# Attention's token sums tied three a step behind the evacuation, and one weight split five steps later

## The chip, the core and the metric

The kernel runs on one core of a Trainium2 chip. The metric is the device time of one execution in microseconds (us). The core has TensorE (matrix products, PE in the rows), VectorE (DVE), ScalarE (ACT), GpSimd (POOL) and SyncE (SP), which issues most DMA transfers. Each engine works through its own list of instructions in order; an instruction waits for those on other engines that it depends on, and all behind it on its engine wait with it.

## What is computed

Causal attention with a decay, then a layer of four weighted two-layer networks, then a gated two-layer network, all in float32:

```python
B, H, S, D = 2, 8, 576, 64
scores = q @ k.T / sqrt(D) + (cum[:, None] - cum[None, :])   # cum = cumsum(log(clip(f, 1e-4, 1))), causal mask
x = softmax(scores) @ v                                     # to tokens: (1152, 512)
p = domain_probs / domain_probs.sum(-1)
x = sum(p[:, e] * (relu(x @ w1[e]) @ w2[e]) for e in range(4))   # w1: 512 x 1024, w2: 1024 x 512
h = x @ w_in                                                # 512 x 2048
out = (h * sigmoid(1.702 * h)) @ w_out                      # 2048 x 512
```

## The kernel before

Each float32 operand of a product is split into a rounded high part and a low part (`whi`/`wlo` for weights, `xh`/`xl` for tokens, `hh`/`hl` for hidden values, `th`/`tl` for token sums, `sh`/`sl` for weight sums), and a product is made of three: high by high, low by high, high by low. ScalarE (now and then GpSimd) makes the high part by rounding, VectorE the low part by a subtraction. So the low parts, the softmax maxima, the additions to the accumulators `acc` and the combinations in joint halves all queue on VectorE.

The work is a list `seq` of units in *visits*. A visit is one half of one expert's hidden width, with its weights `a` (first layer, 4 splits) and `b` (second layer, 4 splits). Kind 1 is a first layer over one chunk of tokens (line 934, evacuated to `hh` and `hl` by line 1087 and 1088), kind 2 a second layer (line 1099, evacuated into `acc` by line 1141 or 1143). Kinds 3 and 7 are *joint* halves (`emit_joint`, line 974): the first layer over two chunks at once with seven products instead of eight, which needs sums of tokens (`ts`, `ts_rest`) and of weights (`ws`). Visits 0 to 6 run while attention is still going; from visit 7 (`v_exp`) on there are joint halves. In visits 11 to 13 (`both_joint`) there are two joint kinds: 3 over the later 640 tokens and 7 over the first 512 (the "rest"). In each such visit the units come in the order (3, first half), the second layer over the rest of the visit before, (7, 0), (3, second half), (7, 1), (2, ...).

The main loop (line 1329 on) walks through the steps of these units. In a step it emits the products of this step, pulls some steps of the generator `attention()` (scores, maxima, exponentials, norms, transposes, products with v), emits the evacuation of the step before (`evac[0]()`), and then low parts, weight splits and whatever the table of `place()` puts at this step. The list of loads is worked off on SP with four buffers (`wst`), each filled again when its pair of splits is done.

Two kinds of token sums matter here. `rest_sums` (line 336) makes the sums for the rest, tokens 0 to 511, that is attention's first batch. It runs in two halves of 256 columns. In each are four sums, made by two or three additions on VectorE (line 362, into `rsa` or `rsb`), a rounding on ScalarE and a subtraction on VectorE (line 355, into the one buffer `rs`), and a store to DRAM on SP (`tsd`, line 357); they are read back some 100 us later. Each instruction is one `yield`. `sum_tokens` (line 307) makes the sums for tokens 512 to 1151, `th` and `tl`, with additions at line 330 (into `tr`) and subtractions at line 325; they need the last tile of attention (`xl`, line 765), and the first joint half of visit 7 needs them.

A sum of the rest is emitted through `in_turn`, which ties it to the instruction of the same engine emitted just before it: it stays behind that one. The order on each engine is otherwise made by the scheduler, from these ties and from readiness by its own estimates; from visit 7 on `pin_turn` keeps the written order on VectorE, ScalarE and GpSimd. `late_by` counts steps from 3 down from the first step in which the rest's sums may run; they are pulled from the fourth on, two between the attention steps of a step (where there are any) and one behind the evacuation. What is left when attention ends is emitted at once (`for _ in rest_gen[0]`).

Of the kernel before, what the change touches and what calls it, by code (L numbers as in the profile page):

```python
# [50 lines left out]
def attn_moe_mlp(ctx: ExitStack, tc: tile.TileContext, qk0, qk1, qk2, v0, vp, fg, dp, wa_moe, wb_moe, wa_mlp, wb_mlp, out):  # L51
# [36 lines left out]
    late = {}  # L88
# [687 lines left out]
    def in_turn(fn, *args):  # L776

        block = nc.cur_bb.bb.instructions
        n, prev = len(block), {}
        for i in block:  # L780
            prev[i.engine] = i
        fn(*args)
        for i in block[n:]:
            if i.engine in turn_engines:
                if i.engine in prev:
                    tc.add_manual_dep(i, prev[i.engine].name,
                                      mybir.DependencyInfo(mybir.DependencyClass.NoSync, mybir.DependencyReason.DATA),
                                      reason="in_turn")
                prev[i.engine] = i
# [428 lines left out]
    def pull():  # L1218
        d = next(att, None)
        pulled[0] += 1  # L1220
        if d is not None:
            ready[0] = d
# [42 lines left out]
    def steps(kind, v_, b, c):  # L1265
        if (kind, v_) == (2, v_exp - 1) and c == NCH - 1:
            return len(tiles(c)) - OVER
        return {1: 4, 2: len(tiles(c)), 3: 7, 4: 10 - OVER, 5: OVER, 6: OVER, 7: 7}[kind]
# [17 lines left out]
    def place():  # L1286

        at = {}

        def put(u, g, what, *args):  # L1290
            at.setdefault((u, g), []).append((what, args))

        for v_ in range(v_exp, v_all):
            b, (c1, c2) = visits[v_]
            h0, h1, l2 = (3, v_, b, c1), (3, v_, b, c2), (4, v_, b, c1)
            put(h0, 1, sum_weights, v_ + 1, 0)
            put(h1, 1, sum_weights, v_ + 1, 1)
            for u, m in ((l2, 0), ((5, v_, b, c1), 1)):
                put(u, -0.5, high_sums, v_ + 1, m)
                put(u, 0, low_sums, v_ + 1, m)  # L1300
            first = v_ == v_exp
            places = [(h1, 5), (h1, 6)] + [(l2, i) for i in range(1, 7)]
            if first:
                put((6,) + units[-1], -0.5, high_sums, v_, 1)
                put((6,) + units[-1], 0, low_sums, v_, 1)
                nxt0 = (3, v_ + 1, visits[v_ + 1][0], c1)
                places = [(h0, 0), (h0, 1)] + places + [(nxt0, 0), (nxt0, 1)]
            todo = [("b", v_)] * first + [("a", v_ + 1), ("b", v_ + 1)]
            for (kind, w_, g), (u, i) in zip([(*t, g) for t in todo for g in range(4)], places):
                put(u, i, split_w, kind, w_, g)  # L1310
        for v_ in range(v_all, v_mlp):
            b, (c1, c2, _) = visits[v_]
            h0, h1, l2 = (3, v_, b, c1), (3, v_, b, c2), (2, v_, b, c1)
            more = v_ + 1 in both_joint
            if v_ == v_all:
                mid = (1, v_, b, REST)
                put(h1, 0, load_rest_sums)
                put(h0, 1, sum_weights, v_ + 1, 0)
                put(mid, -0.5, high_sums, v_ + 1, 0)
                put(mid, 0, low_sums, v_ + 1, 0)  # L1320
                put(mid, 1, sum_weights, v_ + 1, 1)
                continue
            r0, r1 = (7, v_, b, 0), (7, v_, b, 1)
            put(r0, -0.5, split_rest)
            put(r0, 5.5, high_sums, v_, 1)
            put(h1, -0.5, low_sums, v_, 1)
            if more:
                put((2, v_ - 1, b - 1, REST), 2, sum_weights, v_ + 1, 0)
                put(r1, 5, sum_weights, v_ + 1, 1)
                put(r1, 6, high_sums, v_ + 1, 0)  # L1330
                put(l2, 0, low_sums, v_ + 1, 0)
            fill = (2, v_ - 1, b - 1, REST)
            for k, (u, i) in enumerate([(fill, 3), (fill, 3), (r0, 1), (h1, 2)]):
                put(u, i, split_w, "b", v_, k)
            for g in range(4):
                put(l2, g, split_w, "a", v_ + 1, g)
        return at

    def split_sums_done():
        if sum_due:  # L1340
            sv, sm = sum_due[0][:2]
            if (sv, 0) in j_done if sm else sv - 1 not in joint or (sv - 1, 1) in j_done:
                split_sums()

    place_at = place()
    pin_units = [u for u in seq if u[1] in both_joint and (u[1], u[3]) != (v_mlp - 1, REST)] + [u for u in seq if u[:2] == (2, v_all) and u[3] == REST]
    evac = [lambda: None]
    j_done = set()
    late_by = [3]
    rest_gen, rest_from = [], seq.index((1,) + units[6])  # L1350
    cv_due = [0]
    in_turn(emit_first, 3, True)
    for i, (kind, v_, b, c) in enumerate(seq):
# [10 lines left out]
        u, m = (kind, v_, b, c), c if kind == 7 else visits[v_][1].index(c)  # L1364
# [13 lines left out]
        for g in range(n_steps):  # L1378
# [21 lines left out]
            n = 0  # L1400
            if nxt:
                j, cc = nxt[0]
                left = sum(steps(*u) for u in seq[i:j]) - g
                n = max(0, -(-(due[cc] - pulled[0]) // left))
                if rest_gen and not late:
                    late_by[0] -= 1
                spread = (n // 3, 2 * n // 3) if late_by[0] < 0 and not late else ()
                for k in range(n):
                    pull()
                    for _ in range(spread.count(k)):  # L1410
                        in_turn(next, rest_gen[0], None)
            rests = []
            for d in split_due[:]:
                d[0] -= 1
# [5 lines left out]
            low_now = lows[:]  # L1420
            lows.clear()
            evac[0]()
            if late_by[0] < 0 and not late:
                in_turn(next, rest_gen[0], None)
            for l_, q, h_ in low_now:
                nc.vector.tensor_sub(l_, q, f(h_))
# [93 lines left out]
```

## Time and profile before

| | us |
|---|---|
| median of 3 runs | 702.58 |
| lowest, highest | 702.44, 703.52 |
| profiled execution, whole | 702.49 |
| its span, first to last instruction | 700.8 |
| TensorE busy in the span | 685.0 (98%) |
| VectorE busy | 533.1 (76%) |
| ScalarE busy | 355.0 (51%) |
| GpSimd busy | 238.1 (34%) |

The profile is that of one execution. Busy time of TensorE is modelled from pipelined products, so 98% does not mean that each product comes at its full pace; the start-to-start distance of products tells that. The mean granted clock over the span is 0.998 of full speed. Attention takes the span up to about 190 us, the plain halves of experts run beside and behind it, joint halves from 215 us on, the last network from about 500 us.

### The profile page before, as it was taken

Reading aid. Unit: us, or ns where it says so; the run is one execution under the profiler, and the core shown is the slowest. Engines: PE = TensorE matmul, PEld = TensorE weight load, DVE = VectorE, ACT = ScalarE, POOL = GpSimd, SP = SyncE. Lnnn points to the kernel's source line nnn. Section 1 sums busy time; section 2 is a strip of 40 time slices with the busy share of each in tenths; the row PEclk is TensorE's granted clock in tenths of the full one; section 3 lists DMA queues with packets and bytes.
Section 4 is the critical chain, followed back from the end, with each engine's and each line's share of the span. In section 5 each row is a group of like instructions: output and inputs, shape, how many; then the busy total and the mean of one; then the engine's idle time right before and its main releaser. Section 6 shows DMA issues by size and latency. Waiting matters only on the chain. (4 is left out here: it accounts for less than half of the span.)

```text
span 700.8 us, 11093 instructions
## 1 busy us (share of the span) xinstructions
PE 685.0 (98%) x3936; PEld 601.5 (86%) x3937; DVE 533.1 (76%) x1097; ACT 355.0 (51%) x821; POOL 238.1 (34%) x286
## 2 busy tenths in 40 slices
PE   8999999999997999999999999999999999999997
PEld 4797888888796888988889898898899898998986
DVE  6896776676478787686996887876889989988632
ACT  5777766676532465454237245253357355453520
POOL 6887566632202645544035235122103220120000
PEclk9999999999999999999999999999999999999999
DMA  8786735400542041244540341432331543441012
GB/s 250 232 294 241 270 114 193 127 31 1 210 151 91 31 151 59 106 122 163 158 140 36 121 121 30 151 106 76 121 105 47 155 159 122 158 158 60 1 46 90
DMA packets 41063, 87.59 MB, mean 125 GB/s; under 512 B 3720, under 2 KB 5776, under 8 KB 40752
## 3 DMA queue, kind: packets, MB, share of 16 engines
q1 hardware_dynamic: 40680, 84.75, 36.6%
q0 software_dynamic: 288, 2.10, 0.8%
q8 instruction: 31, 0.51, 0.3%
q14 instruction: 24, 0.20, 0.1%
q10 hardware_dynamic: 40, 0.04, 0.0%
HBM read 73.98 MB, written 12.88 MB: 124 GB/s over the span
## 5 line engine op out<-in xcount | busy, mean ns | idle before, releaser
L1099 PE MATMUL m<-whi,hh 128*128 128x512 f32 x392 | 110.6, 395 | 0.0
L1099 PE MATMUL m<-wlo,hh 128*128 128x512 f32 x392 | 109.1, 392 | 0.0
L1099 PE MATMUL m<-whi,hl 128*128 128x512 f32 x392 | 107.5, 390 | 0.0
L249 DVE TENSOR_TENSOR wlo<-wst,whi 128x512 fp32r<-128x512 f32 x132 | 100.7, 777 | 7.6 <-ACT whi L71 7.0
L985 POOL TENSOR_TENSOR hl<-jc,hh 128x320 fp32r<-128x320 f32 (+1 forms) x60 | 52.2, 872 | 142.2 <-ACT hh L71 142.2
L71 ACT ACTIVATE whi<-wst 128x512 fp32r<-128x512 f32 x136 | 80.8, 625 | 24.5 <-PE m L1099 14.6
L1099 PEld LDWEIGHTS m<-wlo,hh 128*128 128x128 f32 x392 | 73.7, 189 | 15.5
L1099 PEld LDWEIGHTS m<-whi,hl 128*128 128x128 f32 x392 | 73.4, 188 | 15.4
L1099 PEld LDWEIGHTS m<-whi,hh 128*128 128x128 f32 x392 | 72.3, 189 | 12.8 <-issue 0.3
L270 POOL TENSOR_TENSOR sr<-wst 128x256 f32<-128x256 f32 x20 | 18.6, 928 | 170.9 <-DMA wst<-wm 68.5
L708 POOL TENSOR_SCALAR e<-e,sm 128x128 f32<-128x128 f32 (+4 forms) x72 | 46.6, 659 | 53.7 <-DVE sm L706 32.1
L983 ACT ACTIVATE jc<-jc 128x320 f32<-128x320 f32 (+1 forms) x60 | 27.1, 451 | 55.7 <-DVE jc L980 55.2
L1143 DVE SCALAR_TENSOR_TENSOR acc<-m,dpn,acc 128x512 f32<-128x512 f32 x63 | 46.4, 743 | 9.1 <-PE m L1099 9.1
L934 PE MATMUL m<-xh,wlo 128*128 128x256 f32 (+2 forms) x256 | 51.4, 313 | 0.0
L934 PE MATMUL m<-xh,whi 128*128 128x256 f32 (+2 forms) x256 | 51.3, 316 | 0.0
L934 PE MATMUL m<-xl,whi 128*128 128x256 f32 (+2 forms) x256 | 50.7, 314 | 0.0
L698 ACT ACTIVATE e<-e,mx 128x128 f32<-128x128 f32 (+4 forms) x72 | 41.6, 580 | 12.9 <-DVE mx L682 12.3
L934 PEld LDWEIGHTS m<-xh,whi 128*128 128x128 f32 x256 | 41.5, 189 | 1.6
L934 PEld LDWEIGHTS m<-xh,wlo 128*128 128x128 f32 x256 | 41.5, 189 | 0.7
L1082 ACT ACTIVATE m<-m 128x384 f32<-128x384 f32 x48 | 23.0, 479 | 37.3 <-DVE m L980 35.6
L934 PEld LDWEIGHTS m<-xl,whi 128*128 128x128 f32 x256 | 41.1, 189 | 0.7
L1012 ACT ACTIVATE u<-m 128x320 f32<-128x320 f32 (+2 forms) x26 | 11.2, 432 | 50.5 <-PE m L974 50.5
(173 smaller groups left out, 1520.0 us busy)
## 6 DMA issues: line engine op xcount, KB each, us to landing
wst<-in_wa_moe_dram SPq DMA_DIRECT2D x28, 512.0 KB, 4.0
wst<-in_wb_moe_dram SPq DMA_DIRECT2D x28, 512.0 KB, 4.4
mst<-in_wa_mlp_dram SPq DMA_DIRECT2D x16, 512.0 KB, 3.8
wm<-wf SPq DMA_DIRECT2D x32, 256.0 KB, 4.0
mst<-in_wb_mlp_dram SPq DMA_DIRECT2D x16, 512.0 KB, 4.3
wst<-wm SPq DMA_DIRECT2D x16, 512.0 KB, 3.9
cb<-cumd SPq DMA_DIRECT2D x16, 256.0 KB, 4.0
qr<-in_qk_dram SPq DMA_DIRECT2D x8, 384.0 KB, 5.2
```

The source lines that it names most:

```text
L71: return nc.scalar.activation(out=out, in_=in_, func=AF.Copy)
L249: (nc.gpsimd if v_ == 0 and kind == 'a' and g < 4 else nc.vector).tensor_sub(lf, raw, f(hf))
L270: nc.gpsimd.tensor_add(r[:, 0], a21, a22)
L698: nc.scalar.activation(out=e[:, off:off + w], in_=e[:, off:off + w], func=AF.Exp, scale=-1.0, bias=mx, accum_out=sm[:, 0, k:k + 1])
L708: nc.gpsimd.tensor_scalar(out=e[:, off:off + w], in0=e[:, off:off + w], scalar1=sm[:, 0, i:i + 1], scalar2=1.0, op0=ALU.mult, op1=ALU.mult)
L934: nc.tensor.matmul(p[:, :n], lhsT=w[:, k, :], rhs=x[c][:, k, :], start=(j == 0 and k == 0), stop=(j == 2 and k == 3))
L983: nc.scalar.activation(out=r, in_=r, func=AF.Relu)
L985: nc.gpsimd.tensor_sub(hl[:, g, :], r, f(hh[:, g, :]))
L1012: nc.scalar.activation(out=u[0], in_=pa[:, :WN], func=AF.Copy)
L1082: nc.scalar.activation(out=p[:, :n], in_=p[:, :n], func=AF.Gelu_apprx_sigmoid)
L1099: nc.tensor.matmul(p, lhsT=h_tile(v_, b, c, j, x, k), rhs=wb[v_, k][w].rearrange("p a c -> p (a c)"), start=i == 0 and k == 0, stop=i == 2 ...
L1143: nc.vector.scalar_tensor_tensor(out=a, in0=p, scalar=d, in1=a, op0=ALU.mult, op1=ALU.add)
```

## The change

Two edits. In the main loop the sums of the rest are no longer spread between the pulled attention steps: from the same fourth step on, three are emitted in each step, all behind the evacuation, whether the step pulls attention or not. In `place()` the fourth `b` split of visits 11 to 13 moves from step 2 of (3, second half), `h1`, to step 3 of (7, 1), `r1`.

```diff
             fill = (2, v_ - 1, b - 1, REST)
-            for k, (u, i) in enumerate([(fill, 3), (fill, 3), (r0, 1), (h1, 2)]):
+            for k, (u, i) in enumerate([(fill, 3), (fill, 3), (r0, 1), (r1, 3)]):
                 put(u, i, split_w, "b", v_, k)
...
-                spread = (n // 3, 2 * n // 3) if late_by[0] < 0 and not late else ()
-                for k in range(n):
+                for _ in range(n):
                     pull()
-                    for _ in range(spread.count(k)):
-                        in_turn(next, rest_gen[0], None)
...
             evac[0]()
-            if late_by[0] < 0 and not late:
+            for _ in range(0 if late_by[0] >= 0 or late else 3):
                 in_turn(next, rest_gen[0], None)
```

The first place is VectorE about 153 us into the span, where `hl` of a hidden tile is made between two softmax maxima (line 682); `rsa` is the first running sum of the rest. A piece of the difference:

```order
 L682 ISA mx 128x1
 L1088 SCALAR_TENSOR_TENSOR hl<-m,hh 128x256
+L362 TENSOR_TENSOR rsa<-xh 128x256
 L249 TENSOR_TENSOR wlo<-wst,whi 128x512
 L682 ISA e,mx<-s,cbs 128x288
 L682 ISA mx 128x1
-L705 TENSOR_SCALAR sm<-sm 128x1
+L362 TENSOR_TENSOR rsa<-rsa,xl 128x256
+L705 TENSOR_SCALAR sm<-sm 128x1
+L362 TENSOR_TENSOR rsa<-rsa,xl 128x256
 L706 RECIPROCAL sm<-sm 128x2
 L1088 SCALAR_TENSOR_TENSOR hl<-m,hh 128x256
```

Three additions of the first sum now stand here, where none stood; before, the first of them came 41 rows of this list further on, about 19 us later.

The second place is VectorE around the start of the later sums (`tr`, line 330). Before, the last sums of the rest (`rs`) and the hidden tiles of 384 columns stand directly in front:

```order
L362 TENSOR_TENSOR rsb<-rsb,xl 128x256
L249 TENSOR_TENSOR wlo<-wst,whi 128x512
L355 TENSOR_TENSOR rs<-rsa,rs 128x256
L1088 SCALAR_TENSOR_TENSOR hl<-m,hh 128x384
L249 TENSOR_TENSOR wlo<-wst,whi 128x512
L1141 TENSOR_SCALAR acc_79<-m,dpn 128x512
L355 TENSOR_TENSOR rs<-rsb,rs 128x256
L330 TENSOR_TENSOR tr<-xh 128x640
L330 TENSOR_TENSOR tr<-tr,xl 128x640 x2
L1141 TENSOR_SCALAR acc_2926<-m,dpn 128x512
L285 TENSOR_TENSOR sl<-sr,sh 128x512 x2
L325 TENSOR_TENSOR tl<-tr,th 128x640
```

And now, from attention's last tile (`xl`, line 765) on:

```order
L765 TENSOR_TENSOR xl<-x,xh 128x320
L1088 SCALAR_TENSOR_TENSOR hl<-m,hh 128x256
L362 TENSOR_TENSOR rsb<-rsb,xl 128x256 x2
L1143 SCALAR_TENSOR_TENSOR acc_79<-m,dpn,acc_79 128x512
L355 TENSOR_TENSOR rs<-rsb,rs 128x256
L330 TENSOR_TENSOR tr<-xh 128x640
L330 TENSOR_TENSOR tr<-tr,xl 128x640
L1143 SCALAR_TENSOR_TENSOR acc_79<-m,dpn,acc_79 128x512
L330 TENSOR_TENSOR tr<-tr,xl 128x640
L285 TENSOR_TENSOR sl<-sr,sh 128x512 x2
L1088 SCALAR_TENSOR_TENSOR hl<-m,hh 128x384
L325 TENSOR_TENSOR tl<-tr,th 128x640
```

The sums of the rest end right behind attention's last tile, and `tr` stands ahead of all four hidden tiles of 384 columns instead of behind them.

On TensorE at the first joint half, before (`m<-xh` are its first products, `m<-th` those with token sums, line 1099 second layers of the visit before):

```order
L1099 MATMUL m<-whi,hh 128x512
L1099 MATMUL m<-wlo,hh 128x512 x4
L1099 MATMUL m<-whi,hl 128x512 x4
L1099 MATMUL m<-whi,hh 128x512 x3
L974 MATMUL m<-xh,whi 128x320 x2
L974 MATMUL m<-xh,wlo 128x320 x2
L974 MATMUL m<-xl,whi 128x320
L1099 MATMUL m<-whi,hh 128x512
L1099 MATMUL m<-wlo,hh 128x512 x4
L1099 MATMUL m<-whi,hl 128x512 x4
L974 MATMUL m<-xl,whi 128x320
L974 MATMUL m<-th,sh 128x320 x2
L974 MATMUL m<-th,sl 128x320 x2
```

And now:

```order
L1099 MATMUL m<-whi,hh 128x512 x4
L1099 MATMUL m<-wlo,hh 128x512 x4
L1099 MATMUL m<-whi,hl 128x512 x4
L1099 MATMUL m<-whi,hh 128x512 x4
L1099 MATMUL m<-wlo,hh 128x512 x4
L1099 MATMUL m<-whi,hl 128x512 x4
L974 MATMUL m<-xh,whi 128x320 x2
L974 MATMUL m<-xh,wlo 128x320 x2
L974 MATMUL m<-xl,whi 128x320 x2
L974 MATMUL m<-th,sh 128x320 x2
L974 MATMUL m<-th,sl 128x320 x2
L974 MATMUL m<-tl,sh 128x320 x2
```

All second layers but the last two tiles' worth now stand ahead of the first joint product, instead of between its parts.

The third place is VectorE in the second joint half of visits 11 to 13 and the half behind it (`u`, lines 1017 and 1020, and `jc`, line 980, are the combinations of products in a joint half; 320 columns in kind 3, 256 in kind 7). Before:

```order
L1017 TENSOR_TENSOR u_4578<-m,u_4578 128x320
L249 TENSOR_TENSOR wlo<-wst,whi 128x512
L1020 TENSOR_TENSOR u_4579<-m,u_4578 128x320
L980 TENSOR_TENSOR jc<-m,u_4579 128x320
L980 TENSOR_TENSOR jc<-u_4579,m 128x320
L980 TENSOR_TENSOR jc<-m,u_4578 128x320
L1045 SCALAR_TENSOR_TENSOR hl<-m,hh 128x320
L1017 TENSOR_TENSOR u_4651<-m,u_4651 128x256
L1020 TENSOR_TENSOR u_4652<-m,u_4651 128x256
L980 TENSOR_TENSOR jc<-m,u_4652 128x256
L980 TENSOR_TENSOR jc<-u_4652,m 128x256
```

And now:

```order
L1017 TENSOR_TENSOR u_4578<-m,u_4578 128x320
L1020 TENSOR_TENSOR u_4579<-m,u_4578 128x320
L980 TENSOR_TENSOR jc<-m,u_4579 128x320
L980 TENSOR_TENSOR jc<-u_4579,m 128x320
L980 TENSOR_TENSOR jc<-m,u_4578 128x320
L1045 SCALAR_TENSOR_TENSOR hl<-m,hh 128x320
L1017 TENSOR_TENSOR u_4645<-m,u_4645 128x256
L1020 TENSOR_TENSOR u_4646<-m,u_4645 128x256
L980 TENSOR_TENSOR jc<-m,u_4646 128x256
L249 TENSOR_TENSOR wlo<-wst,whi 128x512
L980 TENSOR_TENSOR jc<-u_4646,m 128x256
```

`wlo` has left its place between the two `u` of 320 columns and stands between the third and the fourth combination of the 256-column half.

## Rows read from the trace of the kernel before

**Rows 1.** TensorE's waits: engine, line, waited for: us in total, times, longest us
```profile
PE m L974 <- ACT th L71: 4.4, 1, 4.4
PE m L974 <- DVE jc L980: 2.1, 4, 0.9
```

**Rows 2.** Stretches: length, busy us of each engine, then granted clock, DMA share, GB/s
```profile
62.00:66.00 4.00, 4.00 (x31) 3.82 (x32) 3.27 (x10) 4.00 (x13) 1.16 (x2) 1.00 1.02 365
157.65:195.00 37.35, 37.01 (x255) 31.50 (x254) 21.97 (x69) 21.60 (x60) 9.01 (x15) 1.00 0.28 99
215.28:244.04 28.76, 22.76 (x119) 19.76 (x117) 24.30 (x33) 9.47 (x20) 14.25 (x15) 0.94 0.19 64
222.79:226.89 4.10, 4.09 (x13) 3.49 (x13) 3.26 (x4) 0.74 (x1) 0.57 (x1) 0.58 0.34 128
```

**Rows 3.** TensorE's timeline: start us, us, instruction [idle before <-releaser]
```profile
61.90 0.33 PE L726 MATMUL t<-identr,e 128*128 128x128 f32 x1 [1.45 <-POOL e L708]
...
206.30 0.85 PE L934 MATMUL m<-xh,whi 128*128 128x384 f32 x4
206.99 0.85 PE L934 MATMUL m<-xh,wlo 128*128 128x384 f32 x4
...
215.28 0.45 PE L974 MATMUL m<-xh,whi 128*128 128x320 f32 x2
215.57 0.46 PE L974 MATMUL m<-xh,wlo 128*128 128x320 f32 x2
...
217.17 1.07 PE L1099 MATMUL m<-whi,hl 128*128 128x512 f32 x4
218.07 0.30 PE L974 MATMUL m<-xl,whi 128*128 128x320 f32 x1
222.79 0.85 PE L974 MATMUL m<-th,sh 128*128 128x320 f32 x2 [4.42 <-ACT th L71]
...
244.04 0.63 PE L1099 MATMUL m<-tsh,hh 128*128 128x512 f32 x2
```

**Rows 4.** VectorE's timeline, 164 to 220
```profile
164.92 0.56 DVE L682 CUSTOM_DVE_ANT_0 e<-s,cb 128x384 f32<-128x384 f32 x1
...
172.60 0.42 DVE L362 TENSOR_TENSOR rsa<-xh 128x256 f32<-128x256 f32 x1
...
188.71 0.49 DVE L765 TENSOR_TENSOR xl<-x,xh 128x320 fp32r<-128x320 f32 x1 [3.21 <-ACT xh L71]
...
201.68 0.75 DVE L1143 SCALAR_TENSOR_TENSOR acc<-m,dpn,acc 128x512 f32<-128x512 f32 x1 [1.98 <-PE m L1099]
...
209.35 0.55 DVE L1088 SCALAR_TENSOR_TENSOR hl<-m,hh 128x384 fp32r<-128x384 f32 x1
...
214.23 0.81 DVE L330 TENSOR_TENSOR tr<-xh 128x640 f32<-128x640 f32 x1
...
217.43 1.28 DVE L285 TENSOR_TENSOR sl<-sr,sh 128x512 fp32r<-128x512 f32 x2
...
219.37 1.34 DVE L330 TENSOR_TENSOR tr<-xh,tr 128x640 f32<-128x640 f32 x1
```

**Rows 5.** ScalarE's timeline, 206 to 223
```profile
206.77 0.42 ACT L71 ACTIVATE rs<-rsb 128x256 fp32r<-128x256 f32 x1 [3.17 <-DMA tsd<-rs]
...
222.01 0.74 ACT L71 ACTIVATE th<-tr 128x640 fp32r<-128x640 f32 x1 [4.46 <-DVE tr L330]
```

**Rows 6.** GpSimd's timeline, one of four weight sums with VectorE's additions elsewhere
```profile
189.22 0.73 POOL L270 TENSOR_TENSOR sr<-wst 128x256 f32<-128x256 f32 x1 [10.47 <-DMA wst<-in_wa_moe_dram]
```

**Rows 7.** TensorE's and VectorE's timelines around two joint halves
```profile
421.52 0.46 PE L974 MATMUL m<-xl,whi 128*128 128x320 f32 x2
422.38 0.56 PE L974 MATMUL m<-xh,sh 128*128 128x320 f32 x2 [0.40 <-DVE jc L980]
...
420.49 0.81 DVE L249 TENSOR_TENSOR wlo<-wst,whi 128x512 fp32r<-128x512 f32 x1 [0.56 <-ACT whi L71]
...
475.53 0.42 DVE L980 TENSOR_TENSOR jc<-u,m 128x256 f32<-128x256 f32 x1 [0.56 <-PE m L974]
```

## The prediction, made before the changed kernel was run

> **What bounds the kernel now.** I began with what TensorE waits for, since it is the engine that is hardly ever idle. Of all its waits one stands out: 4.4 us, once, for a rounding on ScalarE, and next come four waits of 2.1 us together for an addition on VectorE [rows 1]. So the second step was to find the places in time, and the table of stretches shows that one of them is far poorer than the rest. From 215.28, where the first product of the first joint visit begins, to 244.04 TensorE is busy 22.76 of 28.76 us, at a mean clock of 0.94 [rows 2]. Its timeline gives the detail [rows 3]: the product that reads `th` could have started at 218.2 and starts at 222.79.
>
> What that place costs in all is read from its own pace. A matrix product of 320 columns starts 0.147 us after the one before (two in 0.29, from 215.28 to 215.57), one of 512 columns after 0.225 to 0.2275 (four in 0.90, from 217.17 to 218.07). Between 215.28 and 244.04 lie 84 of the first kind and 33 of the second: 84 x 0.147 + 33 x 0.2275 = 19.9 us. They took 28.76, so **8.9 us are lost there**. About 4.6 are the wait itself. Behind it the granted clock is 0.58 on the mean from 222.79 to 226.89 [rows 2], between its two levels of 1.2 and 2.4 GHz (after idling 4.4 us; the wait of 1.45 us that ends at 61.90 was followed by a clock of 1.00 [rows 2, 3]): 4 + 8 products that need 2.4 us took 4.1, which is 1.7 more. The other 2.6 are short waits up to 241 for late additions.
>
> The cause is VectorE's queue. The first of the token sums for attention's first batch (`rsa`) runs there at 172.60, and the last pair only ends at 214.23, where the sums for the next stage begin (`tr`) [rows 4]; ScalarE rounds the second of these at 222.01, having idled 4.46 us for VectorE, and that is the `th` TensorE waits for [rows 5]. These later sums need the tokens of the last attention tile, ready at 189.2 (`xl`, 188.71 + 0.49) [rows 4]. So they start 25 us later than their data allows, behind 18 instructions of the earlier sums.
>
> From 244 on TensorE runs nearly without a break. What is left are three waits of one form, 0.57 us each by start times (421.52 + 0.29 = 421.81, but the next product starts at 422.38) [rows 7].
>
> **The first edit: sums three a step, behind the evacuation.** It adds and removes no work: 28 additions and 8 roundings, 8 stores of 256 KB. What moves is the order. Before, a sum was tied behind the attention work just emitted, thus behind a softmax that runs many steps later. Now it is tied behind an evacuation, which is due at once. The first piece of order above shows the first sums from some 153.5 on instead of 172.60. The DVE time for it is there: 21.97 of 37.35 us are used from 157.65 to 195 [rows 2], and the 12 additions and 6 second parts that stood behind 195, at 0.42 each like the one at 172.60 [rows 4], add up to 7.5 us more: 79%, which VectorE carries, but no longer with room for every wait.
>
> When do the later sums start? In the new order TensorE does nine more 512-column products ahead of the first joint product, 9 x 0.2275 = 2.05 us, so that this one starts at 217.3. Counted back from there, 60 products of 512 columns (13.65), 48 of 384 (0.69 for four, from 206.30 to 206.99 [rows 3]: 8.3) and one of 256 stand between it and the end of attention's last product: 217.3 - 22.1 = 195.2. A rounding and a subtraction later, 1.1 us, `xl` is there: 196.3 where it is 189.2 now, **7 us later**. One evacuation of 0.75 that waits for its tile and four short sums later, `tr` starts at about 199.4, **15 us earlier** than at 214.23. The `th` that TensorE waited for needed 8.5 us from there (214.23 to 222.75). With the five evacuations and weight splits that now stand between (about 3 us) it comes at 210 to 211. It is needed at 218.2, as before: the 0.9 us of products between 217.3 and `th` are the same. **The hole closes, with 7 us to spare**, and the additions behind it are early too: 8.9 us gained.
>
> What is late next? The same queue, in front of the hole. From the evacuation of a finished tile, readable at 201.1 (217.3 less 16.5 of products, and 0.2 of latency), VectorE has 16 instructions up to the low part of the fourth 384-column hidden tile: one at 0.75, six of 640 columns at 0.81, five of 512 at 0.64, four `hl` at 0.55 [rows 4], 11.0 us in all. Each starts some 0.07 ahead of the end of the one before, so that they end 10.0 us later, at 211.1. TensorE reads it at 217.3 - 25 x 0.2275 = 211.6. So without disturbance it just fits. But GpSimd makes four weight sums right behind one of these instructions, and beside those a 640-wide addition took 1.34 instead of 0.81 [rows 4]. Two or three instructions fall under it, 1.1 to 1.6 us: a **new wait of 0.6 to 1.1**. I take 1.1 and another 0.5 for a hidden tile or a weight sum that is just late, 1.6 together; the bounds are 0 and 3. After a wait of that size the row at 61.90 shows no lower clock.
>
> Here one page speaks of the price. The Trainium skill (SBUF — State Buffer, "Who interferes with whom") says that a VectorE instruction with two SBUF inputs and a GpSimd one that reads SBUF exclude each other for a whole instruction. The trace agrees in kind, but the pair costs 0.53 more here and not the whole other instruction, which alone takes 0.73 [rows 6].
>
> The stores move with the sums, on SP. Each now stands between weight loads that were issued together before; a load waits for its store, a store for its sum. The splits that need these loads come at 166 and 186, behind loads that I place at 159 to 175; so I cost this at nothing, and if the cover is gone, a split and the tile behind it are late by what is missing. The two loads of the last stage's weights (`mst`) now stand behind the fourth store. They are held until attention's last scores, and the fifth store follows them; its rounding is needed only at 189.
>
> **The second edit: one weight split moved by five steps.** In three visits the fourth split (`whi` on ScalarE, `wlo` on VectorE) leaves the third step of the joint half in front and goes into the fourth step of the last half. At 420.49 this `wlo` (0.81) stands between two additions that TensorE waits for [rows 7]. Without it they are ready 0.73 earlier, more than the 0.57 that is lost, and TensorE is again the later one by some 0.1. With the slower first product after such a stop (0.1) each is worth 0.6 to 0.67: **2.0 us in three visits**; bounds 0 and 2.0. Where it goes, VectorE waits 0.56 us for TensorE before 475.53 [rows 7]; the split takes 0.61 there and nothing on TensorE hangs on the 0.05. The split is needed 2 us later, by the eighth product of the second layer. The buffer it frees comes 6 us later, and so does one load on SP; nothing is queued behind it for longer than that.
>
> **The sum.** The profiled execution took 702.49 (a span of 700.8 and 1.7 around it), 0.1 less than the median of 702.58. 702.49 - 8.9 + 1.6 - 2.0 = 693.2; against the median, **693.3 us**.
>
> **The rivals.**
> - No new wait at all: VectorE makes the fourth hidden tile in time. 702.6 - 8.9 - 2.0 = 691.7. For it: the sum above fits without GpSimd. Against: no spare.
> - GpSimd's sums exclude VectorE's in full: four instructions of 0.73 [rows 6] then cost VectorE 2.9, the wait is 211.1 + 2.9 - 211.6 = 2.4 instead of 1.1, and the time 694.6. The 1.34 [rows 4] speaks against the full price. (It is the rule of the Trainium skill's page SBUF — State Buffer that was named above.)
> - Attention's tail gets late. The sums now stand ahead of softmax maxima: the one at 164.92 [rows 4] comes behind an evacuation, a rounded pair, a sum and a split, at about 168. Its scaled exponentials are then ready at about 174.7, and by the paces above their transposes come at 177.2, 3.6 us later than in the old order, which leaves 2.5 us; a chain later than that stops TensorE, once or twice, for 3 to 5 us: 696 to 698.5, say 697.
> - The hole stays in part, because attention's last tile is late: 4.4 and 1.7 of the 8.9 are not gained, 699.5.
> - The second edit gives nothing, another addition being as late: 695.3.
> - **Slower than before.** All eight rounded pairs use one buffer, so a rounding on ScalarE waits until the store before has landed. Before 206.77 it waited 3.17 us so [rows 5], at a time when nothing else was due there. Now exponentials, copies of transposes and hidden tiles are queued behind it. Seven such waits that reach TensorE with over 1.5 us each outweigh 10.9. At 2 us each it is 705.7. Against it: most stores now have 4 us or more before the next rounding.
>
> **How the numbers follow.** Chances: forecast (692.2 to 694.5) 0.46; no new wait 0.16; full exclusion 0.07; late tail 0.15; hole in part 0.06; second edit without effect 0.04; slower 0.05; nothing to measure 0.01. The range from 691.0 to 698.0 leaves out slower, the hole in part, and the upper part of the tail, 0.15 in all. A measurement of this kernel can tell 0.2%, some 1.4 us, from no change. Faster 0.93, same 0.02, slower 0.05.
>
> **What would show it.** Right: no wait of TensorE for `th` over 0.5 us and a clock of 1.00 from 215 to 245; `tr` starting before 203; a short wait for `hl` near 211; no wait for `jc` near 370, 415 and 460. Wrong: waits for `t`, `x` or `s` between 160 and 196, or ScalarE idle for `tsd`.

## The result and the profile after

The changed kernel takes **691.82 us** (median of 4 runs, 691.44 to 692.28), where the kernel before, run beside it, takes 702.54 (4 runs, 702.44 to 703.52). The ratio is 0.9845, 95% interval 0.9828 to 0.9862. The span of the profiled execution went from 700.8 to 690.1 us, its mean granted clock from 0.998 to 0.999.

TensorE's three longest waits are now these (the columns are those of [rows 1]). All lie in the first 80 us; from 150 us on no wait of TensorE is left that the view lists.

```profile
PE m L1171 <- DVE acc L1164: 1.9, 1, 1.9
PE t L726 <- POOL e L708: 1.4, 1, 1.4
PE s L652 <- DVE mx L682: 0.9, 1, 0.9
```

The waits of [rows 1] are gone, for `th` and for `jc` alike. The two stretches that answer to [rows 2]:

```profile
157.65:195.00 37.35, 37.35 (x260) 31.80 (x261) 27.45 (x82) 22.62 (x63) 9.87 (x16) 1.00 0.45 143
...
215.28:235.25 19.97, 19.97 (x119) 18.56 (x118) 14.24 (x23) 7.40 (x17) 9.96 (x11) 1.00 0.17 46
```

The second one begins at the same time as the stretch of 28.76 us in [rows 2], ends with the same product (`tsh`, line 1099) and holds as many products, 119. It is as long as the 19.9 us that the prediction worked out from TensorE's pace, at a clock of 1.00. In the first one VectorE does 82 instructions in 27.45 us where it did 69 in 21.97.

TensorE's timeline, against [rows 3]:

```profile
211.08 1.07 PE L1099 MATMUL m<-whi,hl 128*128 128x512 f32 x4
...
216.52 1.07 PE L1099 MATMUL m<-whi,hl 128*128 128x512 f32 x4
...
217.43 0.45 PE L974 MATMUL m<-xh,whi 128*128 128x320 f32 x2
...
218.30 0.46 PE L974 MATMUL m<-th,sh 128*128 128x320 f32 x2
...
235.25 0.63 PE L1099 MATMUL m<-tsh,hh 128*128 128x512 f32 x2
```

The first joint product starts at 217.43, and the product that reads `th` follows at 218.30 without a wait. The product that stood at 244.04 in [rows 3] starts at 235.25.

VectorE's and then ScalarE's timeline, against [rows 4, 5]:

```profile
153.76 0.42 DVE L362 TENSOR_TENSOR rsa<-xh 128x256 f32<-128x256 f32 x1
...
168.28 0.55 DVE L682 CUSTOM_DVE_ANT_0 e<-s,cb 128x384 f32<-128x384 f32 x1
...
195.81 0.49 DVE L765 TENSOR_TENSOR xl<-x,xh 128x320 fp32r<-128x320 f32 x1 [1.03 <-ACT xh L71]
...
199.36 0.82 DVE L330 TENSOR_TENSOR tr<-xh 128x640 f32<-128x640 f32 x1
...
205.20 1.35 DVE L330 TENSOR_TENSOR tr<-xh,tr 128x640 f32<-128x640 f32 x1
...
212.04 0.55 DVE L1088 SCALAR_TENSOR_TENSOR hl<-m,hh 128x384 fp32r<-128x384 f32 x1
...
193.04 0.42 ACT L71 ACTIVATE rs<-rsa 128x256 fp32r<-128x256 f32 x1 [0.87 <-DMA tsd<-rs]
...
209.02 0.74 ACT L71 ACTIVATE th<-tr 128x640 fp32r<-128x640 f32 x1 [0.66 <-DVE tr L330]
```

The sums of the rest begin at 153.76 instead of 172.60; attention's last tile is ready at 196.30; `tr` starts at 199.36 instead of 214.23. The second `th` is rounded at 209.02 instead of 222.01. Of the eight roundings of sums only the seventh waits for a store, for 0.87 us.

### The profile page after: what moved, and what is told of

Same layout as the page of the kernel before. It is cut to its first block, busy times and chain, and to the rows that moved or that the text cites. A ratio compares the mean times of both kernels' runs of the same rounds, so it can differ in the third digit from the quotient of the medians.

```text
span 690.1 us, 11086 instructions
## 1 busy us (share of the span) xinstructions
PE 681.2 (99%) x3937; PEld 600.0 (87%) x3937; DVE 531.4 (77%) x1097; ACT 354.3 (51%) x821; POOL 239.4 (35%) x286
## 4 chain that ended last, share of the span: by engine, by line
PE 92%; DVE 4%; POOL 1%; ACT 1%; DMA 1%; issue 1%; SPq 0%; POOLq 0%; DVEq 0%
PE m L1099 41%; PE m L974 23%; PE m L934 15%; PE s L652 4%; PE x L756 4%; PE t L726 3%; PE m L1255 1%; DMA dpraw<-in_dp_dram 1%; DVE acc L1143 0%; POOL ks L578 0%; DVE hl L1088 0%; DVE cvd L431 0%; DVE wlo L249 0%; PE m L951 0%; DVE wf L433 0%
## 5 line engine op out<-in xcount | busy, mean ns | idle before, releaser
L71 ACT ACTIVATE ph<-t 128x256 f32<-128x256 f32 (+4 forms) x81 | 28.9, 405 | 17.6 <-PE t L726 17.2
```

The lines of the kernel that those rows point to most:

```text
L71: return nc.scalar.activation(out=out, in_=in_, func=AF.Copy)
```

## How runs are compared here

Up to some 150 us all these kernels give TensorE the same products in the same order, and still the profiled executions differ there by up to 1.5 us. So beside the medians I use the part of each profiled span behind one mark: the transposes `t<-identr,e` x2 of line 726 at 150.28 us before and 150.55 us after. The orders part only behind it. Behind it lie 700.8 - 150.28 = 550.5 us before and 690.1 - 150.55 = 539.6 after.

| run | sums of the rest | start of sums | start of `tr` | median us | behind the mark |
|---|---|---|---|---|---|
| before | spread, 1 without attention | 172.60 | 214.23 | 702.54 | 550.5 |
| second edit alone | as before | 172.64 | 214.25 | 700.97 | 548.5 |
| place only | behind evacuation, 1 without attention | 153.92 | 211.57 | 698.56 | 546.2 |
| number only | spread, 3 | 173.14 | 206.31 | 695.54 | 543.1 |
| number only, two buffers `rs` | spread, 3 | 172.55 | 206.96 | 696.96 | 545.2 |
| number only, earlier start | spread, 3, from first step | 160.15 | 206.72 | 696.47 | 544.4 |
| two a step | behind evacuation, 2 | 153.69 | 206.17 | 694.55 | 542.3 |
| **after** | behind evacuation, 3 | 153.76 | 199.36 | 691.82 | 539.6 |
| six a step | behind evacuation, 6 | 153.50 | 199.12 | 691.91 | 539.9 |

A sum a step means here one instruction of the sums a step (an addition, a rounding, a subtraction or a store). "Spread" is two between the attention steps and one behind the evacuation; "1 without attention" is one sum in a step that pulls no attention step. All but the first row have the split at its new place. The kernel before, run again beside each group of these, had medians of 702.5 to 703.3.

## The experiments

**Each edit alone.** The changed kernel with the split back at its old place, and the kernel before with the split moved:

```diff
-            for k, (u, i) in enumerate([(fill, 3), (fill, 3), (r0, 1), (r1, 3)]):
+            for k, (u, i) in enumerate([(fill, 3), (fill, 3), (r0, 1), (h1, 2)]):
```

> The first edit alone; the fourth second-layer split stays at the third step of the joint half in front. Theory (the edits are worth what their places in the trace show, 8.8 and 1.9 us, and don't hang on each other): three waits for an addition (jc) of about 0.4 come back, 0.57 to 0.65 us each, and the time is 691.8 + 1.9 = 693.7. Rival (the second edit only gains in the new order, or the difference behind 244 us comes from somewhere else): 691.8, without those waits.

> The second edit alone, the sums of the rest as in the kernel before. Theory: the wait of 4.4 us for th and the lowered clock behind it stay as they are, the three waits for jc go, and the time is 702.5 - 1.9 = 700.6. Rival (an addition behind the one freed is as late): 702.5.

Measured: 693.76 us (ratio to before 0.9867, 0.9854 to 0.9881) and 700.97 (0.9967, 0.9956 to 0.9978). Behind the mark the first edit alone is 1.95 us longer than the changed kernel, the second alone 2.04 shorter than before and 8.9 longer than the changed kernel, with its wait of 4.3 us for `th`. So the edits add up, and are worth 8.9 to 9.0 and 2.0 us.

**The subtraction between two additions.** The low part of the fourth split made twice, at the old place and at the new:

```diff
-            (nc.gpsimd if ... else nc.vector).tensor_sub(lf, raw, f(hf))
+            [(nc.gpsimd if ... else nc.vector).tensor_sub(lf, raw, f(hf)) for _ in range(2 if kind == 'b' and v_ in both_joint and g == 3 else 1)]
```

> The first edit alone (693.76), with the low part of the fourth split made twice over in visits 11 to 13, at its old place between two additions. Theory (this subtraction is what the additions behind it wait for): each of the three waits for jc grows by 0.6 to 0.7, 2.0 us in three visits, 695.7. Rival (something else sets the wait): 693.8 to 694.2.

> The changed kernel, with the low part of the fourth split made twice over in visits 11 to 13, at its new place. Theory (nothing that TensorE waits for hangs on VectorE there): 691.8, no new wait. Rival (the place is only just free): 0.6 us a visit, 693.6.

Measured: 696.79 us at the old place, 691.55 at the new. The three waits for `jc` grew from 0.40 to 1.12 each. TensorE's timeline, with the first edit alone and then with the subtraction made twice:

```profile
413.44 0.57 PE L974 MATMUL m<-xh,sh 128*128 128x320 f32 x2 [0.40 <-DVE jc L980]
...
416.02 0.56 PE L974 MATMUL m<-xh,sh 128*128 128x320 f32 x2 [1.12 <-DVE jc L980]
```

Behind the mark the doubling cost 2.1 us at the old place (the median says 3.0, but this execution was 1.2 us late before the mark) and 0.0 at the new one. This is a cause shown: the additions waited for this subtraction, and at the new place VectorE has at least 0.6 us free.

**Place and number taken apart.** The first edit does two things: it puts all sums behind the evacuation, and it raises their number from one to three in steps that pull no attention step. Each alone:

```diff
-            for _ in range(0 if late_by[0] >= 0 or late else 3):
+            for _ in range(0 if late_by[0] >= 0 or late else 3 if n else 1):
```

and, on the kernel before with the split at its new place:

```diff
-            if late_by[0] < 0 and not late:
+            for _ in range(0 if late_by[0] >= 0 or late else 1 if n else 3):
                 in_turn(next, rest_gen[0], None)
```

> The changed kernel, but in a step that pulls no attention step only one sum is emitted, as in the kernel before; in the other steps three, all behind the evacuation. So the place is the new one and the number the old one. If the place closes the hole: 691.8, tr (line 330) starting near 200. If the number in the steps without attention closes it: as the second edit alone, 700.6, with the wait for th of 4.4 us. My own estimate from the order: the last pair of the sums stands behind all four hidden tiles of 384 columns again, tr starts at 209 to 212, its second rounded sum comes 8.5 us later at 217.5 to 220.5 and is needed at 218.2, so a wait of 0 to 2.3 us and 692 to 695.

> The other half: the sums stay spread between the attention steps as in the kernel before, but a step that pulls none emits three instead of one (the split is at its new step). If the place closes the hole: about 700.6, with the wait for th. If the number does: 691.8. My estimate from the order: tr stands behind the first of the four hidden tiles of 384 columns, starts near 205, th comes at about 213.5, and the hole closes: 691.8 to 692.5.

Measured: 698.56 us with the place alone, 695.54 with the number alone. My estimates, 692 to 695 and 691.8 to 692.5, were both too low. The place alone, TensorE and the stretch behind the wait:

```profile
220.62 0.90 PE L974 MATMUL m<-th,sh 128*128 128x320 f32 x2 [2.00 <-ACT th L71]
...
220.62:224.71 4.09, 4.09 (x13) 3.47 (x13) 3.25 (x5) 0.74 (x1) 0.00 (x0) 0.59 0.33 128
```

`tr` starts within my 209 to 212 and the wait of 2.00 is within my 0 to 2.3, but behind it the clock is 0.59 for 4.09 us. In these TensorE does 4 products of 320 columns and 8 of 512, which at its pace take 4 x 0.147 + 8 x 0.2275 = 2.4: another 1.7 us, as behind the wait of 4.42 before [rows 2]. Then come 0.87 for `jc` and short ones. How much of the time is due to the lower clock is not shown: of this run's four executions two had a mean clock of 1.000 over the span and two 0.998, and they took 698.66 and 698.08 against 698.57 and 698.55 us (more in the last section).

The place alone also settles another question. In the changed kernel TensorE has more second layers ahead of the first joint product than before, and these too could have covered the wait. Here the same ones stand ahead, with the first joint product at 217.58, and `th` is waited for all the same. So it is the earlier `tr` that the wait hangs on.

The number alone, ScalarE and TensorE:

```profile
202.05 0.42 ACT L71 ACTIVATE rs<-rsa 128x256 fp32r<-128x256 f32 x1 [3.37 <-DMA tsd<-rs]
...
227.34 0.56 PE L974 MATMUL m<-tl,sh 128*128 128x320 f32 x2 [0.47 <-DVE tl L325]
...
230.52 0.56 PE L974 MATMUL m<-xh,sh 128*128 128x320 f32 x2 [0.87 <-DVE jc L980]
```

The wait for `th` is gone, with `tr` at 206.31, but the end of the same chain is late: 0.47 for `tl`, 0.87 for `jc`. And the sums themselves run into their one buffer: ScalarE stood 3.37 us for a store before the seventh rounding.

**Is it the buffer, or the start?** Two runs on the number alone: a second buffer `rs`, and an earlier start.

```diff
-            t = room.tile([128, 2, SA], F32R, tag="rs", name="rs")
+            t = room.tile([128, 2, SA], F32R, tag="rs", name="rs", bufs=2)
```

```diff
-    late_by = [3]
+    late_by = [0]
```

> The sums spread as before with three in steps without attention (695.54, where ScalarE waited 3.4 and 1.8 us for stores before the seventh and the eighth rounding), and two buffers rs instead of one (for its room one of eight small buffers of the softmax is left out). Theory (the one buffer holds the last sums back, and with them tr, which started at 206.3): tr starts at 200 to 202, the short waits behind 226 go, and the time is 691.8 to 692.5. Rival (the order in which the sums are emitted is what matters, whatever the buffers): 695.5.

> The sums spread between the attention steps as in the kernel before, three also in steps without attention (695.54), but from the first step in which they may run on instead of the fourth. It tells whether the place behind the evacuation is worth something by itself or only through the earlier start of the sums (153.8 instead of 173.1). By the order tr stands ahead of all four hidden tiles of 384 columns, as in the changed kernel. Theory (start and pace are all): tr starts at 199 to 202, no wait behind it, 691.8 to 692.5. Rival (a tie behind softmax steps holds the sums up wherever they start, or the single buffer and the loads on SP do): tr at 205 or later and 694 to 695.5.

Measured: 696.96 and 696.47 us, where the number alone took 695.54, and `tr` at 206.96 and 206.72. Both theories fell: while the sums stay spread, neither a second buffer nor a start 13 us earlier brings `tr` forward. With two buffers the kernel is slower (696.37 to 697.13 against 695.47 to 695.84). Of the earlier start that can't be said: its four executions took 695.10 and 695.32, at a mean clock of 1.000, and 697.62 and 697.96, at 0.997, and the profile is that of 697.62. The earlier start, VectorE, SP, ScalarE, TensorE, and the stretch behind the wait:

```profile
205.26 0.43 DVE L355 TENSOR_TENSOR rs<-rsb,rs 128x256 fp32r<-128x256 f32 x1 [1.33 <-ACT rs L71]
...
177.60 0.82 SPq L400 DMA_DIRECT2D mst<-in_wa_mlp_dram  x2
...
181.97 0.38 SPq L357 DMA_DIRECT2D tsd<-rs  x1
182.40 1.01 SPq L77 DMA_DIRECT2D wst<-in_wb_moe_dram  x2
...
188.12 1.15 ACT L71 ACTIVATE whi<-wst 128x512 fp32r<-128x512 f32 x2 [2.94 <-DMA wst<-in_wb_moe_dram]
...
188.80 1.02 PE L1099 MATMUL m<-whi,hh 128*128 128x512 f32 x3 [1.79 <-ACT whi L71]
...
188.80:192.88 4.08, 4.08 (x11) 3.09 (x12) 2.10 (x4) 1.59 (x4) 0.00 (x0) 0.63 0.46 117
```

The sums then take from 160.15 to 205.69, 45.5 us for the same 36 instructions that took 33 us from 173.14. What is new in both runs is a wait of 1.79 us on TensorE for a split weight (`whi`), whose load was late. Here SP issued nothing from 178.42 on until the store at 181.97 had its sum, and ScalarE waited 2.94 us for the load behind that store. That is the cover that the prediction costed at nothing for the changed kernel, and here it is gone. With two buffers, SP, ScalarE, TensorE, and the stretch behind the wait:

```profile
177.29 0.46 SPq L77 DMA_DIRECT2D wst<-in_wb_moe_dram  x1
...
182.42 0.42 ACT L71 ACTIVATE rs<-rsa 128x256 fp32r<-128x256 f32 x1 [1.15 <-DMA tsd<-rs]
...
184.17 1.15 ACT L71 ACTIVATE whi<-wst 128x512 fp32r<-128x512 f32 x2 [0.84 <-DMA wst<-in_wb_moe_dram]
...
184.85 1.02 PE L1099 MATMUL m<-whi,hh 128*128 128x512 f32 x3 [1.79 <-ACT whi L71]
...
184.85:188.50 3.65, 3.65 (x18) 2.35 (x20) 1.70 (x3) 1.93 (x7) 0.00 (x0) 1.00 1.01 280
```

Here the load was issued at 177.29, no later than in the kernel before (177.33), and still ScalarE waited 0.84 us for it; why it landed late is not shown. The third rounding still waits 1.15 for a store, but ScalarE's waits for stores fell from 7.9 us in all, with the number alone, to 1.2, and `tr` came no earlier. TensorE had by then lost 1.79 us, and 1.18 more for attention's last tile (`xl`), so where `tr` would be without these stays open. How much of the 3.5 us between the number alone and the changed kernel is the buffer and how much the place of the sums on VectorE stays open too; in the runs made here, only with sums behind the evacuation, three or more a step, does `tr` start within 3.1 us of attention's last tile.

**Other rates.** Two and six sums a step behind the evacuation:

```diff
-            for _ in range(0 if late_by[0] >= 0 or late else 3):
+            for _ in range(0 if late_by[0] >= 0 or late else 6):
```

> The changed kernel with two sums a step instead of three. By the order the last pair of sums stands behind the second of the four hidden tiles of 384 columns, so that tr starts at 206 to 208 instead of 199.4 and the th that is needed at 218.2 comes at 214 to 217. Theory (only what is later than that reaches TensorE): the wait for th stays away, waits of 0.3 to 0.9 us for tl, jc and sl behind 226 come as in the run with the sums spread (695.5), 694 to 696. Rival: 691.8, there being enough cover; or 699 if the wait for th comes back.

> The changed kernel with six sums a step behind the evacuation instead of three. Theory (the number only has to end the sums before attention's last tile; more of them in front of softmax maxima costs nothing while the queue has room): they end earlier, tr still waits for attention's last tile, 691.8. Rival (late tail: additions and stores close together hold maxima and ScalarE up, so that TensorE waits for t, x or s between 155 and 196): 1 to 5 us more, 693 to 697.

Measured: 694.55 and 691.91 us. With two a step `tr` starts at 206.17, and again not `th` but what hangs on the end of the chain is late:

```profile
226.20 0.56 PE L974 MATMUL m<-tl,sh 128*128 128x320 f32 x2 [0.47 <-DVE tl L325]
...
229.39 0.55 PE L974 MATMUL m<-xh,sh 128*128 128x320 f32 x2 [0.87 <-DVE jc L980]
```

With six a step the last sum ends at 191.84, ahead of attention's last tile, so `tr` starts no earlier than with three. And the stores are close: ScalarE, then TensorE:

```profile
186.11 0.42 ACT L71 ACTIVATE rs<-rsa 128x256 fp32r<-128x256 f32 x1 [4.07 <-DMA tsd<-rs]
...
191.57 0.74 PE L934 MATMUL m<-xh,whi 128*128 128x256 f32 x4 [1.06 <-DVE hl L1088]
```

Behind a rounding that waits 4.07 us for its store, four split weights and a hidden tile are queued on ScalarE, and soon after TensorE waits 1.06 for the low part of a hidden tile. That is how the prediction's "slower" rival would come about, once and small; behind the mark it is 0.4 us, and the medians, 691.91 and 691.82, don't tell the two apart. Of the three numbers tried, three a step is the smallest that ends in time.

**The one buffer in the changed kernel.** The same second buffer `rs` there, with the order of every engine unchanged:

> The changed kernel with two buffers rs; the order of every engine is the same. Theory (its stores are far enough apart): the one wait of ScalarE for a store, 0.87 us at 193.04, goes, and the time stays at 691.8. Rival (the one buffer costs time somewhere in attention): 690 to 691.

Measured: 692.66 us (691.85 to 693.14); behind the mark 539.5 against 539.6, so no gain. This execution was 1.2 us late before the mark, ahead of the first sum, where the second buffer isn't used yet; from 10 to 30 us its clock was 0.91 on the mean, where the changed kernel's was 1.00. (One small buffer of the softmax less belongs to this run too.)

**Who reads the fourth hidden tile.** In the changed kernel the fourth `hl` of 384 columns ends at 212.59, and the products with `hl` that start at 211.08 did not wait for it. The prediction had them as its readers. To see the true ones, its low part is written ten times over:

```diff
-                nc.vector.scalar_tensor_tensor(out=l_, in0=q, scalar=0.0, in1=f(h_), op0=ALU.max, op1=ALU.subtract)
+                [nc.vector.scalar_tensor_tensor(out=l_, ...) for _ in range(10 if n == 384 and v_ == v_exp - 1 and g == 3 else 1)]
```

> The changed kernel, with the low part of the fourth hidden tile of 384 columns (hl) written ten times over, 0.5 us each, nine of them behind each other and behind other work, so that its last writing ends at 217 or later. It tells who reads it. If the products with hl that start at 211 read it, as the prediction has it, they wait for 5 us or more and the time is 697 or more. If it is only the third tile behind it (products with hl at 216.5): no wait at 211 and 213.8, and the time is 691.8 plus what the 4.6 us of added work do to the sums behind, 0 to 4.

Measured: 696.51 us (two executions), 4.5 more than the changed kernel behind the mark and a little above my 0 to 4. TensorE, VectorE's last three writings, and the stretch behind TensorE's wait:

```profile
211.29 1.07 PE L1099 MATMUL m<-whi,hl 128*128 128x512 f32 x4
...
214.02 1.07 PE L1099 MATMUL m<-whi,hl 128*128 128x512 f32 x4
...
216.74 0.84 PE L1099 MATMUL m<-whi,hl 128*128 128x512 f32 x3
...
226.82 0.39 PE L1099 MATMUL m<-whi,hl 128*128 128x512 f32 x1
...
231.24 0.68 PE L974 MATMUL m<-xh,sh 128*128 128x320 f32 x2 [2.68 <-DVE jc L980]
...
222.18 1.73 DVE L1088 SCALAR_TENSOR_TENSOR hl<-m,hh 128x384 fp32r<-128x384 f32 x3
...
231.24:235.24 4.00, 4.00 (x16) 4.00 (x17) 3.03 (x6) 3.74 (x9) 1.45 (x2) 0.57 0.31 118
```

The last writing ends at 223.91. The four products at 211.29 and the four at 214.02 run without a wait, so they don't read it. Of the third tile, at 216.74, only three are left in their place: the scheduler has moved the one that reads this tile behind the writings, to 226.82. (The fourth of each of the two tiles behind it has been moved too.) So the first reader is the fourth product of the third tile, which in the changed kernel starts at about 216.52 + 3 x 0.2275 = 217.2, 4.6 us after the tile is ready. (The 2.68 us before 231.24 come from elsewhere: with the moved products a tile is finished later, its evacuation stands ahead of `u` and `jc` on VectorE, and `jc` is late. Again the clock behind such a wait is low, 0.57.)

## Why the prediction was right, and the term that was wrong

The time came out 1.5 us below the 693.3 predicted, within the range; the rival "no new wait", 691.7, is what happened. That rival had the right number for another reason: it took VectorE to make the fourth hidden tile by 211.6. The tile came at 212.59, 1.0 later, and no wait came of it because its reader is later still.

- **Bottleneck and cause.** Right. The 8.9 us that TensorE lost between 215.28 and 244.04 are the 8.9 to 9.0 that the first edit brings. The sum is shown, its parts are not: the 1.7 us for the low clock and the 2.6 us of short waits behind it are no separate terms (last section). A count is off as well, without harm: between 189.2 and 214.23 the earlier sums have 20 instructions on VectorE (14 additions, 6 subtractions), not 18.
- **The positions of the order.** Right: first sum at 153.76 (forecast 153.5), first joint product 217.43 (217.3), `xl` ready at 196.30 (196.3), `tr` 199.36 (199.4), second `th` ready at 209.76 (210 to 211). VectorE's share from 157.65 to 195 is 27.45 of 37.35 us, 73% (79%): 11 instructions of the sums more stand in the stretch than before, not 18.
- **The new wait: 1.6 forecast, nothing measured.** This is the mis-sized term, and nearly all of the error. VectorE's side was right: the fourth hidden tile ended at 212.59, within the 212.2 to 212.7 that 211.1 and 1.1 to 1.6 for GpSimd make. The step that failed is "TensorE reads it at 211.6". I took the first second-layer products behind the hidden tiles for their readers. They belong to the unit before, with 256 columns a chunk, that is two tiles of tokens; the chunk of 384 columns comes behind them. `seq` says so: (2, last visit, previous chunk) precedes (2, last visit, this chunk).
- **GpSimd beside VectorE.** Right in size, wrong in the reading of the rule. Four VectorE instructions ran beside the four weight sums: a `tl` (1.03 us), an addition (1.35), a split (1.22) and another addition (0.90), where they take 0.82, 0.82, 0.68 and 0.82 undisturbed. That is 1.4 us more in all, within the 1.1 to 1.6. VectorE's and GpSimd's timelines (the addition of 1.35 at 205.20, between these two, is shown above):

```profile
204.24 1.03 DVE L325 TENSOR_TENSOR tl<-tr,th 128x640 fp32r<-128x640 f32 x1
...
206.48 1.22 DVE L249 TENSOR_TENSOR wlo<-wst,whi 128x512 fp32r<-128x512 f32 x1
...
204.55 1.32 POOL L271 TENSOR_TENSOR sr<-wst 128x256 f32<-128x256 f32 x1
205.84 1.32 POOL L272 TENSOR_TENSOR sr<-sr,wst 128x256 f32<-128x256 f32 x1
```

  From 204.55 on the two engines' instructions end in turn: VectorE at 205.27, GpSimd at 205.87, VectorE at 206.55, GpSimd at 207.16, VectorE at 207.70, each 0.5 to 0.7 us behind the other's, a little less than each takes undisturbed (0.73 for a sum, 0.82 and 0.68 for VectorE's two). So the times fit one engine standing still while the other works, and the 0.53 that the prediction read as a milder price is the rest of the other's instruction. The Trainium skill (SBUF — State Buffer, "Who interferes with whom") states that the ports which VectorE and GpSimd share are an exclusive lock, and that a VectorE instruction with two SBUF inputs contends for them with a GpSimd one that reads SBUF; the trace agrees. What is out is the rival's price: it let VectorE pay for four whole sums, 2.9 us, but parts of the first and the last ran beside an `hl`, which took its usual 0.55 to 0.56. Nothing on TensorE hung on either price.
- **"7 us to spare".** Right for the `th` that was named, wrong as a margin of the place. With `tr` 6.8 us later (two a step) that `th` was not late, but 2.8 us were lost behind the mark, for a later `th`, `tl` and `jc`. In the changed kernel the last `tl` ends at 221.07 and is read at 224.08: 3.0 us are left there.
- **Attention's tail.** Right in place: the maximum forecast at about 168 stands at 168.28, the transposes forecast at 177.2 start at 177.59, without a wait.
- **SP at nothing.** Right here, and no small matter elsewhere: a wait of 1.79 us on TensorE in the run with the earlier start, where a load stood behind a late store.
- **Slower through one buffer.** One wait of 0.87 us instead of seven; a second buffer gains nothing. With six a step the mechanism shows.
- **The second edit.** Right: 2.0 forecast, 1.9 to 2.0 measured. The margin was as thin as forecast. TensorE's and VectorE's timelines after, around the place of the old wait and the new place:

```profile
459.30 0.48 PE L974 MATMUL m<-xh,sh 128*128 128x320 f32 x2
...
458.67 0.49 DVE L980 TENSOR_TENSOR jc<-m,u 128x320 f32<-128x320 f32 x1 [0.44 <-PE m L974]
...
464.15 0.68 DVE L249 TENSOR_TENSOR wlo<-wst,whi 128x512 fp32r<-128x512 f32 x1
```

The addition `jc` ends at 459.16 (458.67 + 0.49), and the product that reads it starts at 459.30, at pace. That is 0.14 us after its input: VectorE has next to nothing to spare there.

## What to carry over

Work that has no urgent reader should be tied to something that is due at once and at a steady pace, and its pace set so that it ends before the work that needs the same queue can begin; where it is tied behind steps that run late, its buffers, stores and the loads behind the stores run late with it. A wait that you forecast needs its reader by name, from the list that orders the program: the next instruction of the right kind is not always the one that reads. The margin of a chain is that of its last link, not of the first one that was seen waiting.

## What was not expected of the chip

TensorE's granted clock after a wait, and what it costs. Behind waits of 4.42, 2.00 and 2.68 us the clock was 0.58, 0.59 and 0.57 on the mean of the next 4 us, between its two levels of 1.2 and 2.4 GHz; behind the one of 1.45 us it was 1.00. Behind a wait of 1.79 us it was 1.00 in one run (two buffers) and 0.63 in another (earlier start). So in these traces the length of a wait does not tell by itself whether the clock falls.

In the stretches behind the waits of 4.42, 2.00 and 2.68 us the products took 1.7 us more than at their pace each time (behind the 2.68, 16 products of 320 columns took 4.00 us where their pace makes 2.35). But that is not what the time lost. In the run of the second edit alone the order is that of the kernel before up to here, the wait is 4.34, and the clock stayed low for longer:

```profile
222.74:228.79 6.05, 6.05 (x16) 5.05 (x17) 5.18 (x6) 0.74 (x1) 2.06 (x3) 0.53 0.23 87
```

Its 4 products of 320 columns and 12 of 512 would take 3.3 us at their pace, so 2.7 are lost there instead of 1.7. Yet the product of line 1099 that ends the stretch starts at 243.99, against 244.04 before: `jc` is then waited for 0.31 us instead of 0.87, and `tl` not at all. VectorE sets the time there, and a slower TensorE waits less for it. The executions of the place alone, as long at a mean clock of 1.000 as at 0.998, point the same way. What the lower clock costs by itself is not shown by these runs.
